# One convolution operation a step earlier, two copies behind a sigmoid, and the sine table loaded at the end of layer 1

## The chip, the core and the metric

The kernel runs on one core of a Trainium2 chip. The metric is device time in microseconds (us) of one execution. The engines are TensorE (PE, with its weight loads PEld), VectorE (DVE), ScalarE (ACT), GpSimd (POOL) and SyncE (SP, which here only issues transfers).

## What is computed

A causal convolution over 7 positions whose weights are a softmax that each position brings along, then two gated layers:

```python
w = softmax(weight_gen)                                   # per token, head: 7 taps
x = sum over k of w[..., k] * x_padded[s + k]             # 2 x 4096 tokens, 192 wide, 8 heads
x = (sigmoid(x @ w_gate) * (x @ w_val)) @ w_out           # layer 1: 192 -> 1536 -> 192
h = x @ w_in                                              # layer 2: 192 -> 2048
out = (h * cos(h)) @ w_out2                               #          2048 -> 192
```

Matrices are fp32. The kernel splits each factor into a rounded half (hi, fp32r) and the rest (lo), and sums three products: hi·hi, lo·hi and hi·lo.

## The kernel before

**Tiles and segments.** The 8192 tokens are cut into 16 chunks of 512. A chunk's pass through layer 1 is a segment of 12 steps (1, c), through layer 2 one of 8 steps (2, c). `LEAD = 2` sets the order: (1,0), (1,1), then (2,0), (1,2), (2,1), (1,3) and so on to (2,13), (1,15), (2,14), (2,15). So from (2,0) on one segment of each layer alternates; I call such a pair, 20 steps, a period.

**A step.** A step of layer 1 is one slice of 128 of the 1536 columns. PE computes the gate and the value into two PSUM banks (`hidden`, L442, 18 matmuls, tile `ph`). ACT takes the sigmoid (`gate`, L578), DVE multiplies (`product1`, L581), ACT copies the product as hi (`halves`, L619, tile `gh`), POOL subtracts for lo (L620, `gl`), and PE multiplies both into the output's four banks (`out_matmuls`, L461, tile `po`, 10 matmuls), some steps later (`waiting`, `OUTS`). `ps_h` has four banks, two steps' worth: the `ph` matmuls of step j + 2 can start only when `product1` of step j has read its bank. A step of layer 2 has two slices and no gate: it reduces the angle (L592, L595 on DVE; L599 on ACT, L600 on DVE), takes the sine (`cosine`, L605, ACT), multiplies (L609, DVE) and splits as above; it too has 18 `ph` matmuls and 20 for the output. The banks of its step j are free for step j + 2 when its second L609 is done.

I write sig4 for the sigmoid of a layer-1 segment's step 4, p4 for its product (L581), ph4 for its matmuls, gh4 and gl4 for its halves.

**What sets the order.** The program is written out in order (`tc.manual_schedule()`), and each engine works its own list from front to back. In a layer-1 step k the list is: `run(pending)` (p and gh, gl of the step before), `do_side` (side work that is due), the matmuls `mm_hidden`, at `j == FINAL` (4) one step of `finish2`, an output product, the sigmoid, `run(late)`.

**Side work.** The convolution of chunk c runs on DVE inside segment (1, c-1), 14 operations: 7 products (L282, tiles `pr` and `acc`, 128x768) and 6 sums (L308, `acc`) with one empty turn. For c = 3 to 15 the table `TAPS` says how many of them are due in each step: the first list is for most chunks, the second for the one chunk with softmax group 2, c = 3. They stand in DVE's list between p of the step before and p of the step itself. Softmax operations (L236 to L246) are spread in the same way.

**Output.** `finish2` brings layer 2's result out: first the sums of the banks (L470, L471), at step 4 of the next layer-1 segment two copies of half a tile on ACT (L504, `vs`) and two adds on POOL (L505, `vc`), later transposes (L507, L511) and transfers.

**The end of a layer-1 segment.** For most chunks `blocks_ops` follows step 11: the convolved chunk is transposed on DVE (L395) and split into `hb` (ACT, L402) and `lb` (POOL, L404), which transfers bring into place as `xT`, the input of the next layer-1 segment. Three chunks (0, 1 and 2) and the last are transposed on PE instead.

**Tables.** ACT holds one table of functions at a time; sigmoid, exponential and sine have one each, the plain copy goes with any. A load (`ACT_TABLE_LOAD`) is put by the compiler in front of the first activation that needs another table. `warm` is a 128x1 tile that is written only to bring such a load about.

Of the kernel before, what the change touches and what calls it, by code (L numbers as in the profile page):

```python
# [13 lines left out]
AF = mybir.ActivationFunctionType  # L14
# [15 lines left out]
def dyn_conv_glu_cos_mlp(  # L30
# [11 lines left out]
    nc = tc.nc  # L42
# [43 lines left out]
    sin_bias = const.tile([P, 1], F32, name="sin_bias")  # L86
    warm = const.tile([P, 1], F32, name="warm")
# [207 lines left out]
    def conv_ops(c):  # L295
        acc = acc_tile()
        att[c] = [acc]
        tap(c, 0, acc)
        last = None
        for k in range(1, K + 1):  # L300
            yield
            if k < K:
                pr = product_tile()
                tap(c, k, pr)
                if last is not None:
                    yield
            if last is not None:
                nc.vector.tensor_tensor(out=acc, in0=acc, in1=last, op=ALU.add)  # L308
            last = pr
# [60 lines left out]
    def transpose_ops(srcs, c):  # L370

        p = banks("pt")
        for n, src in enumerate(srcs):
            transposes(p, src, n == 0, n == len(srcs) - 1)
        xt = xT[1, c] = tpool.tile([P, 2, NQ, N], F32R, name="xT", tag="xB")
        yield
        yield from split_input(xt, p, False)
# [13 lines left out]
    def blocks_ops(c):  # L391

        src = att[c][0]
        tr = product_tile()
        nc.vector.transpose(  # L395
            out=tr.rearrange("p t d -> p (t d)").rearrange("p (b t r) -> p b t r", t=TC, r=BL),
            in_=src.rearrange("p t (b r) -> p b t r", r=BL),
        )
        yield
        hi = apool.tile([P, TC, D], F32R, name="hb", tag="pr", bufs=2)  # L400
        lo = apool.tile([P, TC, D], F32R, name="lb", tag="acc", bufs=1)
        nc.scalar.activation(out=hi, in_=tr, func=AF.Copy)  # L402
        yield
        nc.gpsimd.tensor_tensor(out=lo, in0=tr, in1=hi.bitcast(F32), op=ALU.subtract)  # L404
        xt = xT[1, c] = tpool.tile([P, 2, NQ, N], F32R, name="xT", tag="xB")
        for x, piece in (0, hi), (1, lo):
            v = piece.bitcast(F32).rearrange("p t d -> p (t d)").rearrange("p (q e n) -> p q e n", q=NQ, e=2)
            for e in range(2):
                for b in range(P // BL):
                    nc.sync.dma_start(  # L410
                        out=xt[e * BL:(e + 1) * BL, x, :, b * P:(b + 1) * P].bitcast(F32),
                        in_=v[b * BL:(b + 1) * BL, :, e],
                    )
            yield
        low, top = HALVES
        for x in range(2):
            nc.sync.dma_start(out=xt[top, x, 0:2].bitcast(F32), in_=xt[low, x, 1:3].bitcast(F32))
            nc.sync.dma_start(out=xt[top, x, 2].bitcast(F32), in_=xt[low, x, 0].bitcast(F32))
# [71 lines left out]
    def by_blocks(c):  # L490

        return LEAD < c < NCH - 1
# [146 lines left out]
    later, final = [], None  # L639


    TAPS = [1, 1, 2, 2, 0, 2, 1, 1, 1, 2, 1], [0, 0, 0, 2, 0, 2, 2, 2, 2, 2, 2]
    APART = 0, 1, 6, 7, 8, 10, 10
    NWARM = 8
    SOFT, TAPS0, AHEAD = [0,1,2,3,4], [4,5,6,7,8,9,9], 2
# [15 lines left out]
    def add_side(lo, hi, costs, ops):  # L661

        run = lambda: next(ops, None)
        lo, hi = ([v] * len(costs) if isinstance(v, int) else v for v in (lo, hi))
        side.extend((a, b, cost, run) for a, b, cost in zip(lo, hi, costs))

    def do_side(k, budget):
        i = 0
        while i < len(side):
            lo, hi, cst, fn = side[i]  # L670
            if lo > k:
                i += 1
            elif hi > k and cst > budget:
                break
            else:
                side.pop(i)
                fn()
                budget -= cst
# [11 lines left out]
    def cost(n):  # L690
        return 0.06 + 1.05e-3 * n
# [6 lines left out]
    def run(ops):  # L698
        for f in ops:
            f()  # L700
        ops.clear()

    with tc.manual_schedule():
# [30 lines left out]
        for c in range(1, NCH):  # L734
# [21 lines left out]
            else:  # L756
                n, ops = 2 * K, conv_ops(c)
                k0 = at = [seg_start[1, c - 1] + j for j, m in enumerate(TAPS[group_at.get(c) == 2]) for _ in range(m)]
            add_side(k0, at, [cost(TC * D)] * n, ops)
# [36 lines left out]
        FINAL = 4  # L796
# [5 lines left out]
        def out_products():  # L802
            q = waiting.pop(0)
            q.mm_out()
            return q if q.j == q.nj - 1 else None

        for k, st in enumerate(steps):
            layer, c, j = st.layer, st.c, st.j
            ended = None
            if layer == 1:  # L810
                run(pending)
                do_side(k, 2.5 if k < J1 else 2.0 if k < seg_start[2, 1] else 0.5)
                st.mm_hidden()
                if j == FINAL and final:
                    next(final)
                old = bool(waiting) and (waiting[0].layer, waiting[0].c) != (layer, c)
                if old or len(waiting) >= 2 and OUTS[j]:
                    ended = out_products()
                st.gate()
                run(late)  # L820
                pending.append(st.product1)
                pending.append(lambda st=st: st.halves(0))
                if ended:
                    ended.finish()
                if k in inputs and by_blocks(inputs[k]):
                    blocks = blocks_ops(inputs[k])
                    next(blocks)
                    next(blocks)
                    pending.pop(0)()
                    out_products()  # L830
                    pending.pop(0)()
                    out_products()
                elif k in inputs:
                    c1 = inputs[k]
                    ops = transpose_ops(att[c1], c1)
                    pending.pop(0)()
                    next(ops)
                    if c1 == 1:
                        next(decoding)
                        run(late)  # L840
                    next(ops)
                    out_products()
                    pending.pop(0)()
                    for _ in ops:
                        pass
                    out_products()
            else:
                st.mm_hidden()
                if blocks and next(blocks, blocks) is blocks:
                    blocks = None  # L850
                n = sum(q.layer == 1 for q in waiting)
                for _ in range(-(-n // (2 - j)) if n else len(waiting) >= 2):
                    ended = out_products() or ended
                if final:
                    for at in (0, 0, 3) if c < NCH - 1 else (2, 3, 4, 5):
                        if j == at and next(final, final) is final:
                            final = None
                st.reduce(ended and ended.finish)
                run(pending)
                st.cosine()  # L860
                for i, r in st.tiles_of():
                    st.product2(i, r)
                    if i == 0 or st is steps[-1]:
                        st.halves(i, r)
                    else:
                        pending.append(lambda st=st: st.halves(1))
                do_side(k, 0.5)
                run(late)
            if todo:
                todo.pop(0).load(nc.sync)  # L870
            waiting.append(st)
            if later and not ended and (k < J1 or k >= s2 or j in (3, 5, 7, 9)):
                if next(later[0], later) is later:
                    later.pop(0)
            if layer == 1 and j == st.nj - 2 and c + 2 < NCH:
                load_x(c + 2)
                if c + 4 in group_at and group_at[c + 4] > 2:
                    load_group(group_at[c + 4], "wf")
            if layer == 2 and c == 0 and j == 5:
                load_group(2, "wf")  # L880
# [35 lines left out]
```

## Time and profile before

| | |
|---|---|
| median of 3 runs | 1231.85 us (1231.69 to 1233.48) |
| the profiled execution | 1231.73 us, of which the span from first to last instruction is 1229.9 us |
| PE busy | 1197.9 us, 97% of the span |
| DVE, ACT, POOL busy | 918.5, 787.6, 761.8 us (75, 64, 62%) |
| chain of work that ended last | PE 73%, DVE 9%, ACT 4%, issue 1% |

The busy time of PE says little on its own, since matmuls overlap. What tells is how far apart their starts are: where PE has all it needs, 18 `ph` matmuls take 2.04 us and 10 output matmuls 1.13 us, and what a stretch takes beyond that is lost. The chain of work that ended last names what PE waited for there.

### The profile page before, as it was taken

What the parts mean: (1) busy time and instruction counts of PE and PEld (TensorE: products, weight loads), DVE (VectorE), ACT (ScalarE), POOL (GpSimd) and SP (SyncE); (2) the same over time, 40 slices, a digit from 0 to 9 for tenths busy, and PEclk for the clock granted to TensorE, in tenths of its full rate; (3) what the DMA queues carried; (4) which work ended last, traced back from release to release, by engine and by line L of the source; (5) the groups of instructions that cost most, each with busy time, mean ns of one, the idle gap of its engine ahead of it and who ended that gap; (6) DMA issues with size and microseconds to landing.
All of it is one profiled execution on the core that took longest, in us unless ns stands there. A gap on an engine that the chain in (4) does not pass through costs nothing.

```text
span 1229.9 us, 26781 instructions
## 1 busy us (share of the span) xinstructions
PE 1197.9 (97%) x10624; PEld 991.1 (81%) x10624; DVE 918.5 (75%) x1274; ACT 787.6 (64%) x1299; POOL 761.8 (62%) x573
## 2 busy tenths in 40 slices
PE   6899999999999999999999999999999999999997
PEld 5678878878888888888888888887888888888885
DVE  7957888787887777787777787876877777682676
ACT  6766847558485665847557485665847657485675
POOL 3968756656575565746556665565757557565573
PEclk8999999999999999999999999999999999999998
DMA  9912104132140411303132140312313132020011
GB/s 250 243 51 76 38 13 96 29 80 45 36 88 2 103 33 53 72 33 66 27 95 40 38 87 4 88 33 58 70 33 65 27 82 42 1 57 2 14 28 26
DMA packets 97246, 71.41 MB, mean 58 GB/s; under 512 B 57444, under 2 KB 80994, under 8 KB 97120
## 3 DMA queue, kind: packets, MB, share of 16 engines
q1 hardware_dynamic: 96208, 68.57, 23.8%
q8 instruction: 83, 1.36, 0.5%
q10 hardware_dynamic: 912, 1.13, 0.4%
q14 instruction: 43, 0.35, 0.1%
HBM read 30.33 MB, written 6.29 MB: 30 GB/s over the span
## 4 chain that ended last, share of the span: by engine, by line
PE 73%; DVE 9%; ACT 4%; issue 1%; DVEq 0%; ACTq 0%
PE ph L442 40%; PE po L461 33%; DVE acc L308 4%; DVE wk L581 2%; DVE pr L282 2%; ACT wk L578 1%; ACT gh L619 1%; ACT vs L504 1%; ACT wk L605 0%; DVE wk L592 0%; DVE wk L609 0%; DVE wk L595 0%; DVE vc L471 0%; ACT L578 0%; ACT L241 0%
## 5 line engine op out<-in xcount | busy, mean ns | idle before, releaser
L620 POOL TENSOR_TENSOR gl<-wk,gh 128x512 fp32r<-128x512 f32 x446 | 613.8, 1382 | 430.9 <-ACT gh L619 379.2
L442 PE MATMUL ph<-xT,unit 64*128 64x512 f32 x5760 | 773.0, 389 | 11.6 <-DVE wk L581 9.9
L442 PEld LDWEIGHTS ph<-xT,unit 64*128 64x128 f32 x5760 | 593.3, 184 | 132.7 <-DVE wk L581 18.8
L461 PE MATMUL po<-gh,outu 64*128 64x512 f32 x2688 | 549.9, 387 | 2.1 <-ACT gh L619 1.9
L461 PE MATMUL po<-gl,outu 64*128 64x512 f32 x1792 | 471.0, 388 | 3.2 <-POOL gl L620 3.1
L619 ACT ACTIVATE gh<-wk 128x512 fp32r<-128x512 f32 (+1 forms) x450 | 283.2, 629 | 267.3 <-DVE wk L581 226.5
L461 PEld LDWEIGHTS po<-gh,outu 64*128 64x128 f32 x2688 | 405.6, 184 | 51.4 <-ACT gh L619 2.8
L461 PEld LDWEIGHTS po<-gl,outu 64*128 64x128 f32 x1792 | 317.9, 184 | 37.9 <-POOL gl L620 6.2
L581 DVE TENSOR_TENSOR wk<-ph,wk 128x512 f32<-128x512 f32 x192 | 131.5, 685 | 136.6 <-ACT wk L578 121.9
L609 DVE SCALAR_TENSOR_TENSOR wk<-ph,wk 128x512 f32<-128x512 f32 (+1 forms) x258 | 168.5, 687 | 43.6 <-ACT wk L605 43.6
L605 ACT ACTIVATE wk<-wk,sin_bias 128x512 f32<-128x512 f32 (+1 forms) x258 | 173.0, 713 | 21.0 <-DVE wk L595 10.3
L592 DVE TENSOR_SCALAR wk<-ph 128x512 f32<-128x512 f32 x129 | 88.0, 682 | 66.4 <-PE ph L442 64.9
L578 ACT ACTIVATE wk<-ph 128x512 f32<-128x512 f32 x192 | 113.3, 590 | 32.5 <-PE ph L442 31.2
L599 ACT ACTIVATE wk<-ph 128x512 int32<-128x512 f32 x129 | 75.6, 586 | 79.9 <-PE ph L442 79.1
L308 DVE TENSOR_TENSOR acc<-acc,pr 128x768 f32<-128x768 f32 x78 | 117.5, 1506 | 0.4
L282 DVE TENSOR_TENSOR pr<-xp,sm 128x768 f32<-128x768 f32 x84 | 98.7, 1176 | 0.0
L595 DVE SCALAR_TENSOR_TENSOR wk<-wk,ph 128x512 f32<-128x512 f32 x129 | 88.1, 683 | 4.4
L600 DVE TENSOR_TENSOR wk<-wk,ph 128x512 f32<-128x512 int32 x129 | 87.4, 677 | 0.3 <-ACT wk L599 0.3
L471 DVE SCALAR_TENSOR_TENSOR va<-po,va 128x512 f32<-128x512 f32 x32 | 22.0, 688 | 38.4 <-PE po L461 35.5
L123 POOL TENSOR_TENSOR unit<-wf,unit 128x768 fp32r<-128x768 f32 (+1 forms) x11 | 22.3, 2024 | 13.6 <-ACT unit L121 13.6
L470 ACT ACTIVATE va<-po 128x512 f32<-128x512 f32 x32 | 18.9, 590 | 15.6 <-PE po L461 15.2
L505 POOL TENSOR_TENSOR vc<-vc,vs 64x256 f32<-64x256 f32 x30 | 22.0, 734 | 1.1
(67 smaller groups left out, 492.4 us busy)
## 6 DMA issues: line engine op xcount, KB each, us to landing
xT<-xT SPq DMA_DIRECT2D x78, 256.0 KB, 3.8
xp<-in_x_dram SPq DMA_DIRECT2D x13, 960.0 KB, 4.9
out_dram<-o SPq DMA_DIRECT2D x360, 16.0 KB, 1.5
rawo<-in_moe_w_out_dram SPq DMA_DIRECT2D x7, 768.0 KB, 15.8
xT<-hb SPq DMA_DIRECT2D x96, 48.0 KB, 2.0
xT<-lb SPq DMA_DIRECT2D x96, 48.0 KB, 1.9
raw<-in_moe_w_in_dram SPq DMA_DIRECT2D x8, 384.0 KB, 15.6
xT<-xT SPq DMA_DIRECT2D x24, 128.0 KB, 3.4
```

Of the source, the lines that this page charges most:

```text
L282: nc.vector.tensor_tensor(out=out.rearrange("p t (h g) -> p t h g", g=G), in0=xp[c][:, k:k + TC, :].rearrange("p t (h g) -> p t h g", g=G) ...
L308: nc.vector.tensor_tensor(out=acc, in0=acc, in1=last, op=ALU.add)
L442: nc.tensor.matmul(ps[i], lhsT=u.t[r, w, (s + i) % NQ, c0:c0 + P], rhs=xt[r, x, s, :], start=n == 0, stop=n == len(terms) - 1,)
L461: nc.tensor.matmul(po[2 * i + a], lhsT=w[r, d0:d0 + P], rhs=g[r], start=first and g is gh and d0 < D, stop=last and g is gl,)
L578: nc.scalar.activation(out=self.w[0], in_=self.ps[0], func=AF.Sigmoid)
L581: nc.vector.tensor_tensor(out=self.w[0], in0=self.ps[1], in1=self.w[0], op=ALU.mult)
L592: nc.vector.tensor_scalar(out=w, in0=u, scalar1=0.25, scalar2=ROUND_MAGIC, op0=ALU.add, op1=ALU.add)
L595: nc.vector.scalar_tensor_tensor(out=w, in0=w, scalar=ROUND_MAGIC, in1=u, op0=ALU.subtract, op1=ALU.subtract)
L605: nc.scalar.activation(out=w, in_=w, func=AF.Sin, scale=-SIN_SCALE, bias=sin_bias)
L609: nc.vector.scalar_tensor_tensor(out=w, in0=self.ps[i][:, r], scalar=TWO_PI, in1=w, op0=ALU.mult, op1=ALU.mult)
L619: nc.scalar.activation(out=gh, in_=w, func=AF.Copy)
L620: eng.tensor_tensor(out=gl, in0=w, in1=gh.bitcast(F32), op=ALU.subtract)
```

## The change

Three edits in the function that writes the program.

1. In both lists of `TAPS` one operation is due in step 4 that was due in step 5 (0, 2 becomes 1, 1).
2. At step 4 of a layer-1 segment the step of `finish2` with the copies L504 (and the adds L505 on POOL) is written behind the sigmoid and `run(late)`, not in front of the output product.
3. At the last step of each layer-1 segment (j = 11), behind its sigmoid, a sine of one column is written into `warm`.

```diff
-    TAPS = [1, 1, 2, 2, 0, 2, 1, 1, 1, 2, 1], [0, 0, 0, 2, 0, 2, 2, 2, 2, 2, 2]
+    TAPS = [1, 1, 2, 2, 1, 1, 1, 1, 1, 2, 1], [0, 0, 0, 2, 1, 1, 2, 2, 2, 2, 2]
@@
                 st.mm_hidden()
-                if j == FINAL and final:
-                    next(final)
                 old = bool(waiting) and (waiting[0].layer, waiting[0].c) != (layer, c)
                 if old or len(waiting) >= 2 and OUTS[j]:
                     ended = out_products()
                 st.gate()
                 run(late)
+                if j == FINAL and final:
+                    next(final)
+                if j == st.nj - 1:
+                    nc.scalar.activation(out=warm, in_=sin_bias, func=AF.Sin)
                 pending.append(st.product1)
```

On DVE, in the layer-1 segment that runs from 665 to 705 us, the list from p2 to p6 stood before as follows (L581 is p, L282 a product and L308 a sum of the convolution):

```order
L581 TENSOR_TENSOR wk_9452<-ph_9419,wk_9452 128x512
L282 TENSOR_TENSOR pr_9459<-xp_8722,sm_5643 128x768
L308 TENSOR_TENSOR acc_9308<-acc_9308,pr_9415 128x768
L581 TENSOR_TENSOR wk_9492<-ph_9463,wk_9492 128x512
L581 TENSOR_TENSOR wk_9535<-ph_9500,wk_9535 128x512
L282 TENSOR_TENSOR pr_9542<-xp_8722,sm_5643 128x768
L308 TENSOR_TENSOR acc_9308<-acc_9308,pr_9459 128x768
L581 TENSOR_TENSOR wk_9575<-ph_9546,wk_9575 128x512
L282 TENSOR_TENSOR pr_9582<-xp_8722,sm_5643 128x768
```

and now:

```order
L581 TENSOR_TENSOR wk_9461<-ph_9428,wk_9461 128x512
L282 TENSOR_TENSOR pr_9468<-xp_8730,sm_5648 128x768
L308 TENSOR_TENSOR acc_9317<-acc_9317,pr_9424 128x768
L581 TENSOR_TENSOR wk_9501<-ph_9472,wk_9501 128x512
L282 TENSOR_TENSOR pr_9508<-xp_8730,sm_5648 128x768
L581 TENSOR_TENSOR wk_9540<-ph_9511,wk_9540 128x512
L308 TENSOR_TENSOR acc_9317<-acc_9317,pr_9468 128x768
L581 TENSOR_TENSOR wk_9584<-ph_9555,wk_9584 128x512
L282 TENSOR_TENSOR pr_9591<-xp_8730,sm_5648 128x768
```

One L282 has moved from behind p4 to in front of it; between p4 and p5 only the L308 is left.

On ACT, at steps 3 to 5 of the same segment, before (L578 sigmoid, L619 the hi half):

```order
L578 ACTIVATE wk_9492<-ph_9462 128x512
L619 ACTIVATE gh_9495<-wk_9492 128x512
L504 ACTIVATE vs_9520<-vc_9405 64x256 x2
L578 ACTIVATE wk_9535<-ph_9499 128x512
L619 ACTIVATE gh_9538<-wk_9535 128x512
```

and now:

```order
L578 ACTIVATE wk_9501<-ph_9471 128x512
L619 ACTIVATE gh_9504<-wk_9501 128x512
L578 ACTIVATE wk_9540<-ph_9510 128x512
L504 ACTIVATE vs_9543<-vc_9414 64x256 x2
L619 ACTIVATE gh_9549<-wk_9540 128x512
```

The two copies have changed places with sig4. POOL's list is the same as before, as are PE's and SP's.

On ACT, from sig11 of that segment into the first step of layer 2, before:

```order
L578 ACTIVATE wk_9790<-ph_9760 128x512
L402 ACTIVATE hb_9794<-pr_9792 128x768
L619 ACTIVATE gh_9808<-wk_9790 128x512
L599 ACTIVATE wk_9866<-ph_9823 128x512
L605 ACT_TABLE_LOAD
L605 ACTIVATE wk_9865<-wk_9865,sin_bias_92 128x512
```

and now:

```order
L578 ACTIVATE wk_9799<-ph_9769 128x512
L822 ACT_TABLE_LOAD
L822 ACTIVATE warm_93<-sin_bias_92 128x1
L402 ACTIVATE hb_9804<-pr_9802 128x768
L619 ACTIVATE gh_9818<-wk_9799 128x512
L599 ACTIVATE wk_9876<-ph_9833 128x512
L605 ACTIVATE wk_9875<-wk_9875,sin_bias_92 128x512
```

The load has moved from in front of the first sine to behind the last sigmoid, and `hb` and gh11 stand behind it. In the whole program 15 loads in front of L605 have become 16 in front of `warm`; since (1,0) is followed by another layer-1 segment, one more load of the sigmoid's table stands at the start of (1,1).

## Rows read from the trace of the kernel before

**Rows 1.** The page, part 1: busy time, share of the span, instructions.

```profile
PE 1197.9 (97%) x10624; PEld 991.1 (81%) x10624; DVE 918.5 (75%) x1274; ACT 787.6 (64%) x1299; POOL 761.8 (62%) x573
```

**Rows 2.** Waits of PE, whole span: us in total, times, longest us.

```profile
PE ph L442 <- DVE wk L581: 9.9, 18, 1.0
```

**Rows 3.** Chain of work that ended last, 676 to 694 us: start us, us, what.

```profile
682.63 0.42 ACT vs L504
...
683.51 0.61 ACT wk L578
...
684.89 1.25 DVE pr L282
...
686.22 2.04 DVE acc L308
688.26 0.61 DVE wk L581
...
688.91 2.33 PE ph L442 x17
```

**Rows 4.** Timeline of PE around it: start us, us, what, form, count.

```profile
686.01 2.42 PE L442 MATMUL ph<-xT,unit 64*128 64x512 f32 x19
...
690.86 0.84 PE L461 MATMUL po<-gh,outu 64*128 64x512 f32 x4
```

**Rows 5.** Chain over the whole span, its longest pieces: same place, other periods.

```profile
178.38 2.35 PE ph L442 x17
...
246.86 2.33 PE ph L442 x17
...
1057.23 2.33 PE ph L442 x17
```

**Rows 6.** Timeline of POOL, steps 3 and 4 [idle before <-releaser].

```profile
682.68 1.29 POOL L620 TENSOR_TENSOR gl<-wk,gh 128x512 fp32r<-128x512 f32 x1 [2.22 <-ACT gh L619]
683.94 1.54 POOL L505 TENSOR_TENSOR vc<-vc,vs 64x256 f32<-64x256 f32 x2
685.76 1.68 POOL L620 TENSOR_TENSOR gl<-wk,gh 128x512 fp32r<-128x512 f32 x1 [0.29 <-ACT gh L619]
```

**Rows 7.** Timeline of DVE: p4, an L282 with POOL idle, p7, layer 2's operations.

```profile
684.20 0.69 DVE L581 TENSOR_TENSOR wk<-ph,wk 128x512 f32<-128x512 f32 x1 [2.32 <-ACT wk L578]
...
688.78 0.94 DVE L282 TENSOR_TENSOR pr<-xp,sm 128x768 f32<-128x768 f32 x1
...
693.12 0.68 DVE L581 TENSOR_TENSOR wk<-ph,wk 128x512 f32<-128x512 f32 x1
...
708.86 0.69 DVE L595 SCALAR_TENSOR_TENSOR wk<-wk,ph 128x512 f32<-128x512 f32 x1
...
716.16 0.69 DVE L609 SCALAR_TENSOR_TENSOR wk<-ph,wk 128x512 f32<-128x512 f32 x1 [0.19 <-ACT wk L605]
```

**Rows 8.** Chain, whole span: PE in layer 2's steps 2, 3 and 4.

```profile
270.50 2.09 PE ph L442 x18
...
274.85 2.35 PE ph L442 x18
...
279.47 2.04 PE ph L442 x18
```

**Rows 9.** Timeline of ACT, from sig11 into layer 2 [idle before <-releaser].

```profile
702.62 0.60 ACT L578 ACTIVATE wk<-ph 128x512 f32<-128x512 f32 x1 [0.41 <-PE ph L442]
...
704.10 0.63 ACT L619 ACTIVATE gh<-wk 128x512 fp32r<-128x512 f32 x1
...
708.90 1.28 ACT L605 ACT_TABLE_LOAD   x1
710.19 1.34 ACT L605 ACTIVATE wk<-wk,sin_bias 128x512 f32<-128x512 f32 x2
...
712.27 0.58 ACT L470 ACTIVATE va<-po 128x512 f32<-128x512 f32 x1
```

**Rows 10.** Timeline of ACT at the start of (1,1): its first sigmoid.

```profile
72.25 0.60 ACT L578 ACTIVATE wk<-ph 128x512 f32<-128x512 f32 x1 [1.03 <-PE ph L442]
```

## The prediction

> **What bounds the kernel now.** I read the busy times first, then what PE waits for, then the chain of work that ended last, and last the timelines around each wait. PE is busy for 1197.9 of 1229.9 us and no other engine for more than 919 [rows 1]: PE sets the time, and only what it loses between its matmuls can be won. In the list of its waits one kind stands out, 18 waits for the product L581, 9.9 us in all [rows 2]. In the chain of the whole span 13 of them recur at one place, 17 `ph` matmuls in 2.33 to 2.35 us, from 178.38 to 1057.23 us; the last twelve, (1,3) to (1,14), are 73.67 us apart (1057.23 - 246.86 = 810.37 over 11) [rows 5]. That is one wait in each period.
>
> What it costs is read from the starts, not from the idle time, since a matmul's end overlaps the next one's start. ph6 and ph7 are 36 matmuls and took from 686.01 to 690.86, 4.85 us [rows 4]. Unhindered they take 2 x 2.04 = 4.08 [rows 8]. So 0.77 us is lost here in each period.
>
> The chain at 682 to 689 us tells why [rows 3]. ACT makes the two copies L504 first (from 682.63), then sig4 (683.51). DVE has meanwhile been idle for 2.32 us and starts p4 at 684.20 [rows 7]. Behind p4 it does an L282 and an L308 of the convolution, which end at 688.26, then p5 until 688.95, and ph7 starts at 688.91 (rows overlap by some hundredths). Without a wait ph7 would have started at 686.01 + 2.04 = 688.05. So p5 has to start by about 687.3 for PE not to notice, and it started 0.9 later.
>
> There is a second, smaller loss at the start of layer 2. The `ph` matmuls of its step 2 take 2.09 us and those of step 3 with the outputs before them 2.35, against 2.04 two steps later: 0.05 and 0.31 [rows 8]. It comes 14 times, at the segments (2,0) to (2,13). Step 3 waits for the second L609 of step 1, which ran from 716.16 to 716.85 in the period I follow [rows 7].
>
> **Edit 1, one operation earlier.** No instruction is added. The L282 of step 5 runs in DVE's idle 2.32 us ahead of p4, which begins at 681.88 [rows 7]. POOL has nothing then until gl3 at 682.68 (idle for 2.22 us before it) [rows 6], so I take the duration of an L282 beside an idle POOL, 0.94 [rows 7]: it ends at 682.8, and p4 is not held up, since sig4 comes later. Behind p4 one L308 is left in place of L282 and L308. How long that L308 takes depends on POOL. The L308 of the trace took 2.04 us beside gl4, which ended at 685.76 + 1.68 = 687.44 [rows 3, 6]; it ended 0.82 later. So it waited for POOL and then ran its own time.
>
> The Trainium skill says so too (SBUF — State Buffer, "SBUF: two separate sides"): a VectorE operation with two inputs in SBUF and a GpSimd operation exclude each other for a whole instruction, and whichever starts first holds the port pair. The 0.82 us above agrees; by that rule the moved L282 can also hold up gl3, by 0.1 us. The rule does not tell who follows when both queue, so the sum goes by the bounds below.
>
> **Edit 2, copies behind the sigmoid.** The same two copies, and the same two adds on POOL behind gl3, so nothing is saved in work. sig4 starts when L504 started, 682.63 in place of 683.51, 0.88 earlier, and p4 at 683.3. Behind the copies on ACT stands gh4, which needs p4 and so comes no earlier than they end; POOL's adds begin with gl3's end, 683.94 [rows 6], as before.
>
> Both edits together: p4 ends at 684.0, and L308 is next. Its bounds: POOL has gl3 (until about 684.1), the pair L505 (1.54 us, until 685.6) and gl4 (1.29, until 686.9) one behind the other. If L308 gets in behind gl3, p5 could start at 685.0; behind the first L505 at 685.7; behind both at 686.5; all before 687.3. Only if it has to let gl4 pass too does it end at 686.9 + 0.82 = 687.75, and then 0.45 of the 0.77 us stays. Three of the four orders give all, so I take 0.77: 12 x 0.77 = **9.2 us**. The first of the 13 places is in the segment with the second list, which has two operations each in steps 6 and 7 too; there the wait can only move on to those. Bounds 0 and 0.77 us more, taken 0.6. No other wait of PE stands in the period, and with ph7 on time every later product has its matmuls 0.77 us sooner.
>
> **Edit 3, the table.** 16 loads with their one-column sines replace 15, and (1,1) needs one more. In the trace the load takes 1.28 us from 708.90, and the sine starts at once at 710.19, though its input (L595) was done at 709.55 [rows 7, 9]. With the table in place the sine starts at 709.6: **0.6 us** earlier, not 1.28, since L595 is late next. The second L609 of step 1 comes out up to 0.6 earlier; 0.31 is all that PE lost there. What may stop that is the copy L470, which stands in ACT's list in between (712.27) and waits for an output product of PE; in the trace it just follows its neighbour, so what PE allows is not shown. Bounds 0 and 0.36, taken 0.30, since half of the 0.6 will do: 14 x 0.30 = **4.2 us**.
>
> The load now lies behind sig11, ahead of `hb` and gh11 (704.10) [rows 9], which come some 1.4 us later. ACT has no other work until L599, shortly before 708.90, so this is covered: gh11 ends near 706.1. Queued behind it are gl11 and `lb` on POOL and the transfers of `xT` on SP, with the output transfers behind them; `xT` is read only after all of layer 2's segment, over 30 us later. If that cover were gone it would cost 1.4 us each time. At the start of (1,1) two more loads (2 x 1.28, and 0.2 for the sine) come before a sigmoid that waited 1.03 us for PE [rows 10]: bounds 0 and 1.7, taken 0, since the step after it has its banks already.
>
> The Trainium skill has a dearer load (ScalarE: Activation LUTs, "What ACT_TABLE_LOAD costs"): 1283 ns and about 1380 ns of drain, 2.66 us for each switch. Rows 9 agree with the first part, and show no second: the sine started 0.01 us after the load. By the page the estimate for the two extra loads at (1,1) would be 5.3 us on ACT and gh11 would be later by another 1.4, still behind no wait of PE.
>
> **Sum.** 9.2 + 0.6 + 4.2 = 14.0 us of the profiled execution's 1231.73: 1217.7. The median of the runs lies 0.12 above it, so **1217.8 us**. Lowest, with every loss gone: 12 x 0.77 + 1.2 + 14 x 0.36 = 15.5, 1216.3.
>
> **Rivals.** (a) L308 lets gl4 pass. For it: all four POOL operations are ready in a row. Against: any earlier gap suffices. 12 x 0.45 = 5.4 us stay: 1223.2. (b) The table edit brings nothing, because L470 holds the second L609 where it is: 14.0 - 4.2 = 9.8, 1222.0. For: L470 does wait for PE. Against: it needs only 0.3 of 0.6. (c) The wait moves to ph9, which needs p7. p7 ended at 693.80, and ph9 was due at 690.86 + 1.13 + 2.04 = 694.03: 0.23 us to spare [rows 4, 7]. If p7 stays where it is while PE gains 0.77, 0.54 is lost again, 12 x 0.54 = 6.5: 1224.3. Against: p7 follows p5 and p6, which move up by more than PE does. (d) Slower. The moved L282 gets behind gl3 and L505 on POOL instead of ahead of them: it then ends at 682.68 + 1.29 + 1.54 + 0.82 = 686.3, p4 at 687.0, and ph6, due at 686.01, starts 1.0 late: 1.0 in place of 0.77, 13 x 0.23 = 3.0 us worse. It decides from an L282 that starts 0.8 us later than p3's end. With (b) beside it that is 1234.9; against it stands that DVE is free 0.8 us before gl3. (e) The edits do nothing that counts, because another engine sets p5 at its old time: 1231.9; nothing in the rows does.
>
> **How the numbers follow.** Forecast 0.63, (a) 0.12, (b) 0.12, (c) 0.07, (d) 0.03, (e) 0.03. About 0.2%, 2.5 us, is what a measurement of this kernel can tell from no change. Forecast and (a) to (c) are faster, 0.94; (e) 0.03 the same; (d) 0.03 slower. The range 1216.2 to 1222.6 holds the forecast, (b) and the part of (a) in which less than 0.45 us stays: about 0.8.
>
> **What would show it.** Right: no wait of PE for L581 between (1,3) and (1,14), a period near 72.6 us in place of 73.67, an L282 of about 0.94 us ahead of p4, p5 started by 687.3 on this clock, and 18 `ph` matmuls in 2.04 us in layer 2's step 3. Wrong: ph7 still waiting behind a long L308 (a), L609 of step 1 unmoved (b), a new wait of ph9 (c) or ph6 (d) for L581, or a wait of PE in the first steps of (1,1) for the sigmoid behind the extra loads.

## The result and the profile after

The changed kernel takes **1217.97 us** (1216.89 to 1218.11), beside it on the same chip the kernel before 1232.3 (1231.69 to 1233.48): a ratio of 0.9883, 95% interval 0.9869 to 0.9898. The forecast was 1217.8. The profiled execution took 1217.96 us, its span is 1216.2.

The busy times [rows 1] and the waits of PE for L581 [rows 2] of the changed kernel:

```profile
PE 1191.1 (98%) x10624; PEld 1000.3 (82%) x10624; DVE 911.2 (75%) x1274; ACT 797.6 (66%) x1317; POOL 775.3 (64%) x573
```

```profile
PE ph L442 <- DVE wk L581: 3.6, 6, 1.0
```

The work is the same but for ACT's 18 instructions more (loads and one-column sines). Of 18 waits for a product 12 are gone.

**Where they were.** PE's timeline at ph6 and ph7 of the segment that answers to rows 3 to 7 (start us, us, what, form, count):

```profile
679.08 4.46 PE L442 MATMUL ph<-xT,unit 64*128 64x512 f32 x36
683.15 0.84 PE L461 MATMUL po<-gh,outu 64*128 64x512 f32 x4
...
684.29 4.46 PE L442 MATMUL ph<-xT,unit 64*128 64x512 f32 x36
```

The 36 matmuls take 683.15 - 679.08 = 4.07 us in one piece, where they took 4.85 in two [rows 4]; ph8 and ph9, the last row, are one piece as well. DVE in the same steps (the moved L282, p4, L308, p5; in brackets the idle time before and who ended it):

```profile
674.87 0.94 DVE L282 TENSOR_TENSOR pr<-xp,sm 128x768 f32<-128x768 f32 x1
676.25 0.69 DVE L581 TENSOR_TENSOR wk<-ph,wk 128x512 f32<-128x512 f32 x1 [0.44 <-ACT wk L578]
676.86 1.00 DVE L308 TENSOR_TENSOR acc<-acc,pr 128x768 f32<-128x768 f32 x1
678.83 0.69 DVE L581 TENSOR_TENSOR wk<-ph,wk 128x512 f32<-128x512 f32 x1 [0.97 <-ACT wk L578]
```

The L282 fills DVE's idle time ahead of p4 [rows 7: 2.32 us there], which still is 0.44 us long. p5 now waits 0.97 us for its own sigmoid: nothing on DVE holds it any more. POOL beside it (gl3, the adds) and ACT (sig5):

```profile
675.75 1.29 POOL L620 TENSOR_TENSOR gl<-wk,gh 128x512 fp32r<-128x512 f32 x1 [2.22 <-ACT gh L619]
677.01 2.26 POOL L505 TENSOR_TENSOR vc<-vc,vs 64x256 f32<-64x256 f32 x2
```

```profile
678.14 0.60 ACT L578 ACTIVATE wk<-ph 128x512 f32<-128x512 f32 x1 [0.45 <-PE ph L442]
```

L308 ends at 677.86, 0.82 us behind gl3 (675.75 + 1.29 = 677.04): it waited for gl3 and then ran, ahead of the adds, though these were queued behind gl3. The adds paid for it, 2.26 us in place of 1.54 [rows 6].

**The chain over the whole span**, pieces that answer to rows 5 and 8 (start us, us, what):

```profile
181.86 2.33 PE ph L442 x17
...
244.26 4.08 PE ph L442 x36
...
269.64 2.04 PE ph L442 x18
273.95 2.04 PE ph L442 x18
...
316.79 4.08 PE ph L442 x36
```

A period is 316.79 - 244.26 = 72.53 us, where it was 73.67. Layer 2's steps 2 and 3 (269.64, 273.95) took 2.09 and 2.35 before and 2.04 now. One late piece of 17 is left, at 181.86 in (1,2).

**The end of the segment on ACT** (rows 9): sig11, the load, then (behind the one-column sine, `hb` and gh11) layer 2's L599, its first two sines and the copy L470:

```profile
694.92 0.60 ACT L578 ACTIVATE wk<-ph 128x512 f32<-128x512 f32 x1 [0.78 <-PE ph L442]
695.53 1.28 ACT L822 ACT_TABLE_LOAD   x1
...
700.58 0.60 ACT L599 ACTIVATE wk<-ph 128x512 int32<-128x512 f32 x1 [2.29 <-PE ph L442]
701.88 1.34 ACT L605 ACTIVATE wk<-wk,sin_bias 128x512 f32<-128x512 f32 x2 [0.70 <-DVE wk L595]
...
704.24 0.60 ACT L470 ACTIVATE va<-po 128x512 f32<-128x512 f32 x1 [0.18 <-PE po L461]
```

Behind gh11 ACT still has 2.29 us of idle time: the load is covered. The sine waits for its input L595 and no longer for the load.

### The profile page after: what moved, and what is told of

It is laid out like the page before. It is cut to its first block, busy times and chain, and to the rows that moved or that the text cites. A ratio compares the mean times of both kernels' runs of the same rounds, so it can differ in the third digit from the quotient of the medians.

```text
span 1216.2 us, 26799 instructions
## 1 busy us (share of the span) xinstructions
PE 1191.1 (98%) x10624; PEld 1000.3 (82%) x10624; DVE 911.2 (75%) x1274; ACT 797.6 (66%) x1317; POOL 775.3 (64%) x573
## 4 chain that ended last, share of the span: by engine, by line
PE 84%; DVE 1%; ACT 1%; issue 0%; POOL 0%; DVEq 0%; ACTq 0%
PE ph L442 47%; PE po L461 37%; DVE wk L581 0%; DVE acc L308 0%; ACT gh L619 0%; DVE pr L282 0%; POOL gl L620 0%; ACT wk L605 0%; DVE wk L592 0%; DVE wk L609 0%; DVE wk L595 0%; PE pf L532 0%; DVE wk L600 0%; DVE gl L620 0%; ACT wk L578 0%
## 5 line engine op out<-in xcount | busy, mean ns | idle before, releaser
L442 PE MATMUL ph<-xT,unit 64*128 64x512 f32 x5760 | 764.0, 388 | 5.1 <-DVE wk L581 3.6
L442 PEld LDWEIGHTS ph<-xT,unit 64*128 64x128 f32 x5760 | 599.6, 185 | 112.0 <-DVE wk L581 7.0
L619 ACT ACTIVATE gh<-wk 128x512 fp32r<-128x512 f32 (+1 forms) x450 | 283.1, 629 | 222.6 <-DVE wk L581 188.2
L581 DVE TENSOR_TENSOR wk<-ph,wk 128x512 f32<-128x512 f32 x192 | 131.8, 687 | 135.3 <-ACT wk L578 128.5
L609 DVE SCALAR_TENSOR_TENSOR wk<-ph,wk 128x512 f32<-128x512 f32 (+1 forms) x258 | 168.5, 687 | 33.7 <-ACT wk L605 33.7
L605 ACT ACTIVATE wk<-wk,sin_bias 128x512 f32<-128x512 f32 (+1 forms) x258 | 172.9, 713 | 28.0 <-DVE wk L595 20.4
L578 ACT ACTIVATE wk<-ph 128x512 f32<-128x512 f32 x192 | 113.5, 591 | 60.6 <-PE ph L442 59.7
L599 ACT ACTIVATE wk<-ph 128x512 int32<-128x512 f32 x129 | 75.9, 588 | 63.4 <-PE ph L442 62.6
L282 DVE TENSOR_TENSOR pr<-xp,sm 128x768 f32<-128x768 f32 x84 | 105.9, 1262 | 0.0
L308 DVE TENSOR_TENSOR acc<-acc,pr 128x768 f32<-128x768 f32 x78 | 103.7, 1330 | 0.4
L595 DVE SCALAR_TENSOR_TENSOR wk<-wk,ph 128x512 f32<-128x512 f32 x129 | 88.1, 683 | 4.4
L505 POOL TENSOR_TENSOR vc<-vc,vs 64x256 f32<-64x256 f32 x30 | 31.3, 1044 | 1.9 <-ACT vs L504 0.8
L470 ACT ACTIVATE va<-po 128x512 f32<-128x512 f32 x32 | 19.1, 597 | 19.3 <-PE po L461 19.0
```

The source lines that it names most:

```text
L282: nc.vector.tensor_tensor(out=out.rearrange("p t (h g) -> p t h g", g=G), in0=xp[c][:, k:k + TC, :].rearrange("p t (h g) -> p t h g", g=G) ...
L442: nc.tensor.matmul(ps[i], lhsT=u.t[r, w, (s + i) % NQ, c0:c0 + P], rhs=xt[r, x, s, :], start=n == 0, stop=n == len(terms) - 1,)
L578: nc.scalar.activation(out=self.w[0], in_=self.ps[0], func=AF.Sigmoid)
L581: nc.vector.tensor_tensor(out=self.w[0], in0=self.ps[1], in1=self.w[0], op=ALU.mult)
L595: nc.vector.scalar_tensor_tensor(out=w, in0=w, scalar=ROUND_MAGIC, in1=u, op0=ALU.subtract, op1=ALU.subtract)
L605: nc.scalar.activation(out=w, in_=w, func=AF.Sin, scale=-SIN_SCALE, bias=sin_bias)
```

## The experiments

**One edit at a time.** Three kernels each make one edit of the change in the kernel before; their texts are those lines of the diff alone. First the lists:

```diff
-    TAPS = [1, 1, 2, 2, 0, 2, 1, 1, 1, 2, 1], [0, 0, 0, 2, 0, 2, 2, 2, 2, 2, 2]
+    TAPS = [1, 1, 2, 2, 1, 1, 1, 1, 1, 2, 1], [0, 0, 0, 2, 1, 1, 2, 2, 2, 2, 2]
```

> Edit 1 alone on the kernel before. Theory: PE's wait is for p5, which must start by 687.3 on the clock of before's period; with the L282 ahead of p4, p4 stays at 684.2, L308 comes behind the pair L505 (685.5) and ends at 686.3, so p5 starts at 686.3 and ph7 does not wait: 12 x 0.77 + 0.6 = 9.8 us less, 1222 (1221.5 to 1223.5). Rival: the copies ahead of sig4 are what holds p5, and edit 2 is needed as well: then most of the 0.77 us stays and the time is 1227 or more. The loss at layer 2's step 3 stays at 0.3 us in both.

Measured: 1221.91 us (1221.19 to 1222.64), ratio 0.9919 [0.9904, 0.9934]. The lists alone take ph7's wait away in each period. DVE, p4 to p5, and ph6 in this kernel:

```profile
680.13 0.69 DVE L581 TENSOR_TENSOR wk<-ph,wk 128x512 f32<-128x512 f32 x1 [1.46 <-ACT wk L578]
680.74 1.48 DVE L308 TENSOR_TENSOR acc<-acc,pr 128x768 f32<-128x768 f32 x1
682.14 0.68 DVE L581 TENSOR_TENSOR wk<-ph,wk 128x512 f32<-128x512 f32 x1
```

```profile
681.93 4.46 PE L442 MATMUL ph<-xT,unit 64*128 64x512 f32 x36
```

p4 is as late as before, behind the copies, but one operation follows it.

Then the copies:

```diff
-                if j == FINAL and final:
-                    next(final)
@@
                 run(late)
+                if j == FINAL and final:
+                    next(final)
```

> Edit 2 alone on the kernel before. p4 starts at about 683.3 in place of 684.2; L282 waits for gl3 (684.0) and ends at 684.8. Theory, with VectorE getting in between two queued GpSimd operations as it did in the changed kernel: L308 follows the first L505 and ends at 686.4, p5 starts before 687.3, and the wait goes: 1222 to 1223. Rival: VectorE has to let the second L505 and gl4 pass, L308 ends at 687.7 or later, and 0.45 to 0.77 us of each wait stays: 1228 to 1232.

Measured: 1222.02 us (1221.12 to 1223.11), ratio 0.992 [0.9905, 0.9935]. The copies alone take it away as well. DVE from p4 to p5 in this kernel:

```profile
679.14 0.69 DVE L581 TENSOR_TENSOR wk<-ph,wk 128x512 f32<-128x512 f32 x1 [1.30 <-ACT wk L578]
679.75 1.00 DVE L282 TENSOR_TENSOR pr<-xp,sm 128x768 f32<-128x768 f32 x1
680.68 1.49 DVE L308 TENSOR_TENSOR acc<-acc,pr 128x768 f32<-128x768 f32 x1
682.09 0.68 DVE L581 TENSOR_TENSOR wk<-ph,wk 128x512 f32<-128x512 f32 x1
```

The same list in the kernel before, its first product behind p4 and p5 (the L308 between them took 2.04 us [rows 3]):

```profile
684.81 1.48 DVE L282 TENSOR_TENSOR pr<-xp,sm 128x768 f32<-128x768 f32 x1
...
688.18 0.68 DVE L581 TENSOR_TENSOR wk<-ph,wk 128x512 f32<-128x512 f32 x1
```

Two operations still follow p4, but it comes earlier, and they find POOL freer (1.00 and 1.49 us where the kernel before has 1.48 and 2.04): p5 is as early as with the lists.

Then the table:

```diff
+                if j == st.nj - 1:
+                    nc.scalar.activation(out=warm, in_=sin_bias, func=AF.Sin)
```

> Edit 3 alone on the kernel before. Theory: 14 x 0.30 to 0.36 = 4.2 to 5.0 us less, 1227 to 1228; PE's wait for p5 stays in each period (0.77 us), the 18 matmuls of layer 2's step 3 take 2.04 us, and the extra loads at the start of (1,1) cost nothing. Rival: the extra loads there cost 1.2 us or more, which eats part of it: 1228.5 to 1230.

Measured: 1228.21 us (1227.01 to 1229.24), ratio 0.9968 [0.9958, 0.9978], between what was expected and the rival's time; the table below says more. Layer 2's loss is gone, and the wait of ph7 is where it was (PE's timeline):

```profile
687.74 2.34 PE L442 MATMUL ph<-xT,unit 64*128 64x512 f32 x17 [0.48 <-DVE wk L581]
```

**Lists and table without the copies**, to see whether the copies add anything: the first and the third of these diffs together.

> Edits 1 and 3 without edit 2. Theory: edit 2 is not needed, since with the L282 ahead of p4 p5 starts at 686.3 on the clock of before, 1.0 us ahead of the point at which PE waits: the same time as the changed kernel, 1217.5 to 1218.5. Rival: the later p4 puts L308 behind all of GpSimd's queue and the wait comes back in part: 1220 to 1224.

Measured: 1218.11 us (1216.64 to 1218.73), ratio 0.9887 [0.987, 0.9903]: the time of the changed kernel. So the copies' edit adds nothing that can be measured once the lists are changed. The two ratios alone, 0.9919 x 0.9968 = 0.9887, give it too: lists and table are independent.

The starts of the matmuls say it more sharply. The stretch from the first `ph` matmul of (2,0) to the first of (2,15) holds every place where a wait was to go, and none of the lower clock that some profiles show ahead of it, at 60 us (starts in PE's timelines, us):

| kernel | from | to | takes | saved |
|---|---|---|---|---|
| before | 114.64 | 1180.44 | 1065.80 | |
| lists | 116.09 | 1171.69 | 1055.60 | 10.20 |
| copies | 116.19 | 1171.77 | 1055.58 | 10.22 |
| table | 116.23 | 1177.18 | 1060.95 | 4.85 |
| lists and table | 114.70 | 1165.47 | 1050.77 | 15.03 |
| changed | 115.91 | 1166.71 | 1050.80 | 15.00 |

Lists and table add up (10.20 + 4.85 = 15.05), the copies add nothing to the lists, and the table brings 4.85 us, more than its 3.5 in the medians.

**Both operations in step 4**, the rival that ph6 comes late if DVE has more ahead of p4:

```diff
-    TAPS = [1, 1, 2, 2, 1, 1, 1, 1, 1, 2, 1], [0, 0, 0, 2, 1, 1, 2, 2, 2, 2, 2]
+    TAPS = [1, 1, 2, 2, 2, 0, 1, 1, 1, 2, 1], [0, 0, 0, 2, 2, 0, 2, 2, 2, 2, 2]
```

> The changed kernel with both operations of step 5 due in step 4 (2, 0 in place of 1, 1), so that an L282 and an L308 stand ahead of p4 and none ahead of p5. On the changed kernel's clock p3 ends at 674.95, L282 at 675.8; L308 then races gl3 (675.75) for the port and ends at 676.6 or 677.9. p4 starts by 677.9, ph6 is due at 679.08 and needs p4 done (0.69). Theory: no wait in either order, 1217.5 to 1218.5. Rival (d) of the prediction, VectorE held behind gl3 and the adds L505 ahead of p4: ph6 waits 1 us in each of 13 segments, 1225 to 1231.

Measured: 1216.95 us (1216.67 to 1219.04), ratio 0.988 [0.9865, 0.9895], a little below what was expected and not told apart from the changed kernel. p4 and ph6 (this view ends at 682 us):

```profile
675.49 0.68 DVE L581 TENSOR_TENSOR wk<-ph,wk 128x512 f32<-128x512 f32 x1
```

```profile
677.96 4.24 PE L442 MATMUL ph<-xT,unit 64*128 64x512 f32 x35
```

p4 no longer waits for its sigmoid but for DVE, and it still ends 1.8 us ahead of ph6 (675.49 + 0.68 = 676.17). That the change's single operation makes ph6 late was never near.

**p5 made late again** in the changed kernel, the test of the cause itself: one product of the convolution is computed twice more, with the same result, ahead of p5, and by the second list ahead of p7 in (1,2) (line numbers are 3 higher: L584 is p, L445 the `ph` matmuls).

```diff
+                if k == 4:
+                    for _ in range(2):
+                        tap(c, k, pr)
```

> The changed kernel, with the product of the convolution's step 4 done twice more (the same values) behind the L308 of step 5, that is ahead of p5. On the changed kernel's clock L308 ended at 677.86 and p5 started at 678.83; ph7 was due at 681.12, so p5 may start at 680.4 at the latest. Each repeat takes 0.82 us and waits for GpSimd's L505 and gl4 in between. Theory: p5 starts at 680.9 to 681.5 and PE waits 0.5 to 1.1 us in each of 13 segments: 1224 to 1233. Rival: p5 is not what ph7 waits for (or its room is larger): under 1220.

Measured: 1224.31 us (1223.46 to 1225.98), ratio 0.9938 [0.9923, 0.9953]. An ordinary period, the repeated products, p5 and ph6 with ph7:

```profile
682.78 2.90 DVE L282 TENSOR_TENSOR pr<-xp,sm 128x768 f32<-128x768 f32 x2
685.60 0.68 DVE L584 TENSOR_TENSOR wk<-ph,wk 128x512 f32<-128x512 f32 x1
```

```profile
684.08 4.58 PE L445 MATMUL ph<-xT,unit 64*128 64x512 f32 x36
```

ph7 was due at 684.08 + 2.04 = 686.12; p5 started 0.52 ahead of that, and PE lost 0.12 us against the 4.46 above, less than expected. The extra work used up the time to spare and little beyond, so the expected range holds the time, but not for the reason given. Most of the 6 us come from two places where the same work met a fuller stretch:

```profile
179.72 3.10 PE L445 MATMUL ph<-xT,unit 64*128 64x512 f32 x17 [2.57 <-DVE wk L584]
```

```profile
392.02 2.42 PE L445 MATMUL ph<-xT,unit 64*128 64x512 f32 x19
395.53 2.33 PE L445 MATMUL ph<-xT,unit 64*128 64x512 f32 x17 [1.08 <-DVE wk L584]
397.48 0.84 PE L464 MATMUL po<-gh,outu 64*128 64x512 f32 x4
```

The first is ph9 of (1,2), which waits for p7. From its first `ph` matmul to that of (2,1) this segment takes 46.11 us (146.92 to 193.03), 3.8 more than in the changed kernel (148.10 to 190.38), with a stretch at half the clock in it (granted 0.51 from 181 to 184 us). The second is ph7 of an ordinary segment, (1,5). DVE (L308, p5; between them the repeated pair took 3.45 us) and POOL (the adds, L508 here):

```profile
390.17 1.33 DVE L308 TENSOR_TENSOR acc<-acc,pr 128x768 f32<-128x768 f32 x1
...
394.80 0.68 DVE L584 TENSOR_TENSOR wk<-ph,wk 128x512 f32<-128x512 f32 x1
```

```profile
389.95 2.14 POOL L508 TENSOR_TENSOR vc<-vc,vs 64x256 f32<-64x256 f32 x2
```

Here the first add began ahead of L308 (389.95, 390.17), so that L308 and each repeat had one operation of POOL more ahead of it. What matters for the cause: with p5 late, the wait is back, at the same place, for the same instruction.

What p5 has to spare against ph7 (ph6's start + 2.04, less the 688.91 - 688.18 = 0.73 from p5's start to ph7's in the kernel before), all starts from the timelines above:

| kernel | ph6 | p5 must start by | p5 started | to spare | PE lost |
|---|---|---|---|---|---|
| late p5, (1,5) | 392.02 | 393.33 | 394.80 | -1.47 | 1.38 |
| before | 686.01 | 687.32 | 688.18 | -0.86 | 0.77 |
| late p5, ordinary period | 684.08 | 685.39 | 685.60 | -0.21 | 0.12 |
| lists alone | 681.93 | 683.24 | 682.14 | 1.10 | none |
| changed | 679.08 | 680.39 | 678.83 | 1.56 | none |

Where p5 is late, PE loses what it is late by, less 0.09 us each time. Where p5 is early, nothing is lost.

**The load's cover.** In the changed kernel the table is loaded three times and five times at the segment's end, in place of once, with exponentials between the sines (a switch of tables each):

```diff
-                    nc.scalar.activation(out=warm, in_=sin_bias, func=AF.Sin)
+                    for func in (AF.Sin, AF.Exp, AF.Sin):
+                        nc.scalar.activation(out=warm, in_=sin_bias, func=func)
```

> The changed kernel with three table loads at the end of each layer-1 segment in place of one (sine, exponential, sine), the suspected cost and one more pair. hb and gh11 come 2.9 us later, gh11 ends at 701.2 on the changed kernel's clock in place of 698.3, and L599 starts at 701.2 in place of 700.6. Theory: ScalarE is idle for 2.3 us ahead of L599 and gl11 still ends (702.6) before PE reads it (703.8): 0 to 0.3 us in each of 16 segments, 1218 to 1222. Rival: hb and the transfers behind it are what counts, or a load costs more than the 1.28 us of its row: 1230 and more.

Measured: 1223.49 us (1222.66 to 1224.29), ratio 0.9927 [0.9911, 0.9944], a little above what was expected, and not where it was expected. ACT at the end of an ordinary segment:

```profile
699.55 0.20 ACT L823 ACTIVATE warm<-sin_bias 128x1 f32<-128x1 f32 x1
699.77 1.28 ACT L823 ACT_TABLE_LOAD   x1
...
703.42 0.62 ACT L619 ACTIVATE gh<-wk 128x512 fp32r<-128x512 f32 x1
703.95 0.58 ACT L599 ACTIVATE wk<-ph 128x512 int32<-128x512 f32 x1
```

L599 follows gh11 at once: the idle 2.29 us of the changed kernel are used up, and PE lost nothing in the twelve ordinary segments. The time was lost at three others: the start of (1,1), some 2.6 us; (1,14) to (2,13), some 2.5, where chunk 15's transposes go through PE and their copies on ACT stand behind the loads (PE's wait there is the row below); and 1.1 at 1143 us.

```profile
1072.12 2.97 PE L442 MATMUL ph<-xT,unit 64*128 64x512 f32 x18 [0.79 <-DVE wk L609]
```

With five loads (Sin, Exp, Sin, Exp, Sin):

> The same with five loads: gh11 ends at 704.2 and L599 starts at 704.2, 3.6 us late; gl11 ends at 705.6, 1.8 us behind its matmul. Theory: the cover of some 2.5 to 3 us is used up and 2 to 3.5 us is lost in each of 14 to 16 segments: 1246 to 1272. Rival: PE is still not reached, below 1225.

Measured: 1274.2 us in one execution, a little above what was expected. Now every ordinary segment loses, some 2.9 us by the starts of the matmuls. Twelve of them make 35 of the 56 us; most of the rest stands at the three other places of the kernel with three loads, in part at the lower clock (granted 0.88 from 72 to 100 us). The output products wait for gh11 (and then 0.62 us for gl11):

```profile
731.16 0.73 PE L461 MATMUL po<-gh,outu 64*128 64x512 f32 x4 [0.69 <-ACT gh L619]
```

So the one load of the change has room for two more in a period, but not for four.

**The wait that is left, in (1,2).** Two entries of the second list of the changed kernel exchanged:

```diff
-    TAPS = [1, 1, 2, 2, 1, 1, 1, 1, 1, 2, 1], [0, 0, 0, 2, 1, 1, 2, 2, 2, 2, 2]
+    TAPS = [1, 1, 2, 2, 1, 1, 1, 1, 1, 2, 1], [0, 0, 0, 2, 1, 2, 1, 2, 2, 2, 2]
```

> The changed kernel with two entries of the second TAPS list exchanged, [0,0,0,2,1,1,2,...] to [0,0,0,2,1,2,1,...]: one operation of the convolution moves from step 6 to step 5, so one stands less between p5 and p7 and ph9 of the segment (1,2) no longer waits for p7. Theory (what is left at (1,2) is the same kind of wait, and the second list alone decides it): 0.4 to 0.8 us less than the changed kernel in a profile, no idle of PE for L581 near 182 us; the median some 1217.3, which these rounds can hardly tell from the changed kernel. Rival (p5 or p6 comes late instead, since two more operations now lie ahead of one of them): the wait shows at ph7 or ph8 there, and the time is that of the changed kernel or up to 0.8 us above it.

Measured: 1217.14 us (1216.46 to 1217.47), ratio 0.9876 [0.986, 0.9892]. The expectation named the step wrongly: counted from the segment's first product, the row at 181.86 is ph10, and it waits for p8. PE from ph8 on in this kernel:

```profile
175.94 4.59 PE L442 MATMUL ph<-xT,unit 64*128 64x512 f32 x36
180.14 0.85 PE L461 MATMUL po<-gh,outu 64*128 64x512 f32 x4
...
181.29 2.42 PE L442 MATMUL ph<-xT,unit 64*128 64x512 f32 x18
```

ph10 no longer waits. ph8 and ph9 take 180.14 - 175.94 = 4.20 us in place of 4.08, so ph9 is a little late instead. From its first `ph` matmul to that of (2,1) the segment takes 41.73 us (148.17 to 189.90) in place of 42.28 (148.10 to 190.38). The 0.55 us are seen in the profile and can't be told in the time.

The changed kernel once more, beside it:

> The changed kernel once more, on the same chip as the exchange in the second list. Theory: 1217 to 1218.5 us, and in its profile 17 of the ph matmuls at about 182 us with an idle of some 0.4 us behind L581. A stretch of a few us at the lower clock level may show near 60 us in this profile or not; if it is missing, the span is about 1 us shorter than the 1216.2 us of the first profile.

Measured: 1217.32 us (1216.45 to 1218.14), ratio 0.9878 [0.9864, 0.9893]; the span of its profile is 1215.0 us, and ph10 waits as in the first profile. None of these kernels is faster than the changed one by more than the executions scatter.

## Why the prediction was right

**ph7's wait, 12 x 0.77 = 9.2 us: right**, in size and in cause. It is gone in every period, the lists alone and the copies alone each bring 9.7 to 9.8 us, and with p5 late it comes back. The lists and the copies were costed together; they are two cures of one wait, and either is enough. p5 was 0.86 us late, and each of them moves it by more than that. Their prices don't add.

**p5's place.** It was said to start at 685.0, 1.0 us ahead of ph6 (686.01), if L308 gets in behind gl3. L308 did get in there, and p5 started only 0.25 ahead of ph6 (678.83, 679.08). The step left out that p5 needs sig5 too, and that sig5 waits for PE (0.45 us in the row above). It did no harm, since 1.6 us are left.

**(a), L308 lets gl4 pass: no**, by the 0.82 us behind gl3. The Trainium skill (SBUF — State Buffer, "SBUF: two separate sides") says that a VectorE operation with two inputs in SBUF and a GpSimd operation exclude each other for a whole instruction. The rows agree: L308 ended 0.82 us behind gl3, and the adds took 0.72 longer. Which of two waiting operations goes next is not in it, but the traces tell: the one that started first in the timeline, its wait counted in. In the changed kernel L308 (676.86) stands ahead of the adds (677.01) and goes first; at 390 us of the kernel with the late p5 the first add (389.95) stands ahead of L308 (390.17); in the kernel before gl4 (685.76) stood ahead of L308 (686.22), which had to let it pass. In the twelve profiles 2908 pairs of a convolution operation (L282, L308) and a POOL operation (gl, the adds, `lb`) overlap in time, and in all but one of them, whose starts are 0.02 us apart, the first to start is the first to end. So the rows could have ruled (a) out: with one operation less ahead of it L308 is ready long before gl4.

**(c), the wait moves to ph9: no** in the ordinary segments, by the row of ph8 and ph9 at 684.29. **(d), ph6 late: no**: L282 took 0.94 us and ended 0.44 before p4 started, and even two operations there cost nothing.

**The second list, 0.6 us: right in size, with some luck.** From its first `ph` matmul to that of (2,1) the segment (1,2) took 42.96 us before (147.14 to 190.10) and takes 42.28 now (148.10 to 190.38): 0.68 won. As the prediction had it, the wait moved on; but it went from ph9 (the row at 178.38 in rows 5, which the prediction took for ph7's) to ph10, so the 0.6 was a value between two bounds, set at another step.

**The table, 14 x 0.30 = 4.2 us: right in kind, a little small.** The sine comes as soon as L595 allows, as said, and (b) falls: L470 waited 0.18 us for PE, and the second L609 was early enough nonetheless. Both losses, 0.05 and 0.31, are gone at each place: 14 x 0.35 = 4.9, near the upper bound of 0.36 (the term took 0.30, as the wait of step 3 alone). The table by itself showed less in the medians, 3.5 us, but 4.85 by the starts; the profile of that kernel has the stretch at the lower clock that is told of below, worth 1.2.

**The extra loads at (1,1), taken 0: right.** ACT there, the two loads and the sigmoid of rows 10:

```profile
69.74 1.28 ACT L822 ACT_TABLE_LOAD   x1
...
73.35 1.28 ACT L578 ACT_TABLE_LOAD   x1
74.64 0.60 ACT L578 ACTIVATE wk<-ph 128x512 f32<-128x512 f32 x1
```

PE has no wait for that sigmoid. Two more loads with their sines did bring a wait there (some 2.6 us, above), so the cover is under 3 us. The Trainium skill (ScalarE: Activation LUTs, "What ACT_TABLE_LOAD costs") gives a switch 1283 ns and a drain of about 1380 ns besides. The first agrees with the 1.28 us here. The second is not seen: after a load the sigmoid starts 0.01 us later (73.35 + 1.28, 74.64), and a load starts 0.02 us behind a sine (699.55 + 0.20, 699.77). The measurement decides: 1.28 us. With the Trainium skill's drain the prediction made 5.3 us of the two loads at (1,1), still behind no wait of PE; the wait that two more loads brought speaks against that.

**The sum.** 9.2 + 0.68 + 4.9 = 14.8 us, and the spans differ by 1229.9 - 1216.2 = 13.7. The missing 1.1 us are not in any changed step. They stand at 60 us, ahead of the first changed instruction (69.74). Busy times from 61 to 63 us, with the counts of instructions, in two profiles of the changed kernel, the second that of the repeated run (columns: the stretch, us, PE, PEld, DVE, ACT, POOL, granted clock as a share of 2.4 GHz, share of the DMA engines, GB/s):

```profile
61.00:63.00 2.00, 2.00 (x42) 2.00 (x42) 1.74 (x2) 1.56 (x3) 2.00 (x2) 0.50 0.04 8
```

```profile
61.00:63.00 2.00, 2.00 (x72) 2.00 (x70) 1.72 (x2) 1.59 (x3) 2.00 (x2) 1.00 0.09 31
```

In the first, 42 matmuls in 2 us at 0.50; in the second 72 at 1.00, as in the profile of before. The second has a span of 1215.0, and 1229.9 - 1215.0 = 14.9: the sum. So the forecast's 14.0 was 0.9 short, by the table above all, and the stretch at the lower clock hid most of that in the first profile. In the medians an event of this size lies within the spread of the executions. That the median came out 0.2 us from the forecast is therefore luck in part; the waits and their sizes are not.

## What to carry to other kernels

Work out by when a product must start for the matmuls to run on, and how late it is; then look for the first cure that moves it by that much, since a second cure of the same wait brings nothing (the lists or the copies bring 9.7 to 9.8 us alone; with lists and table in place the copies moved 1218.1 to 1218.0). Costs of DVE and POOL operations that share a port depend on who stands beside them: an operation moved to where POOL is idle costs 0.94 us, beside POOL up to 2.04, and here the one that was ready first went first. A table load is free where its engine idles; more loads in the same place show how much of that is left, and the segments that differ run out first: the ordinary ones here took two more without loss, (1,1) did not.

## What the runs showed of the hardware that I had not expected

The granted clock fell to half (1.2 of 2.4 GHz) for some 3 us at 60 us in six of the twelve profiles and not in the others, and of the changed kernel's two profiles in one, which costs 1.2 us. Ahead of it PE was idle for 1.86 us, waiting for DVE. That alone doesn't decide it: the two profiles of the changed kernel have the same 1.86, and the profile of before has 1.85 and no fall. What else decides is open.
